# Threshold attention followed by a squared-ReLU MLP: order of the first ten attention steps, and value groups of several blocks

## The chip, the cores and the metric

The kernel runs on one core of a Trainium2 chip. The metric is device time in microseconds (us). Before the change it is 1333.52 us, the median of three runs (1333.27 to 1333.55). All data are float32.

## The reference

Attention over 8 batches and 8 heads, 576 rows each, head width 64, and then a two-layer MLP over the 4608 rows that come out (512 wide, 2048 inside):

```python
scores = q @ k.T / 8
scores = where(scores >= max(scores) - tau, scores, -1e9)
attn = exp(scores - max(scores));  attn /= sum(attn) + 1e-9
x = attn @ v                      # (8, 8, 576, 64) -> rows (8 * 576, 8 * 64)
out = maximum(x @ w_in, 0) ** 2 @ w_out
```

The weights w_in and w_out are handed over as 64-bit words and turned into float32 in the kernel.

## The kernel before

**Visits and steps.** Two heads are handled together, one on partitions 0 to 63 and one on 64 to 127 of the transposed queries (`qT`) and keys (`kT`). A visit is one such pair; a step is one block of 128 query rows of a visit (the fifth block, number 4, has 64 rows of each head and makes one tile of 128). The first sweep goes through the four pairs of batch 0 with blocks 0 and 1 only (visits 0 to 3, steps 0 to 7), the second through the same pairs with blocks 2, 3 and 4 (visits 4 to 7, steps 8 to 19). From visit 8 on a visit has all five blocks (visits 8, 9, 10 are steps 20 to 34). From step 35 on another method, by DMA, turns the weights of attention; the change doesn't touch it.

**One step.** `scores` (L258) multiplies on TensorE (L273) into two PSUM pairs, one for each head, and VectorE takes the row maxima (L310). `exponents` (L319) makes a bias and a threshold on ScalarE from both maxima (L322, L323) and then the exponentials of both heads (L325). `threshold` (L328) drops on VectorE what lies below the threshold and sums the rest, reading scores and exponentials (L337), and makes the reciprocal (L339, L340). `divide` (L342) scales on GpSimd (L345, L347). Two steps later `turn` (L378) transposes the tile on TensorE in three parts of three 128-column pieces (L386), each copied to `wT` by ScalarE (L387; for block 4 L393 to L400). Three steps later `mix` (L499) multiplies with the values (L502), 128 query rows (64 for block 4) in a PSUM bank, and ScalarE copies the result to `xT` (L485). The scores of a step use the same PSUM pairs as those of the step before, so its matmuls wait until L337 has read them; only step 1 has a pair of its own.

**Around a step.** `load_qk` (L171) issues ten loads (four for the queries, six for the keys) on SP's queue, `load_v` (L210) four. `prep` (L232) transposes queries and keys on VectorE (L247), one after the other in the last step of the visit before. `round_weights` turns one of 32 weight pieces into float32: stage 0 is two ScalarE instructions (L149, L150), stages 1 and 2 are VectorE (L152, L154), 3 and 4 GpSimd (L156, L158); in the first sweep there is one piece in the first step of each visit from visit 1 on, later one or two in each step. The next load into the area of a piece is issued when the piece is done (L951).

**The MLP in between.** `chunk_at` says at which step 256 rows of `xT` are complete: chunk 0 at step 10. Before that `early()` is true. From then on `fill` inserts MLP pieces (L548, L730) between the attention's instructions on TensorE. `rate` (L885) spreads the 32 pieces of chunk 0 evenly over the steps until all weights are there (`out_from`, step 34), and what comes later over the rest. The order on each engine is the order in which the program issues; an engine does its instructions in that order.

Of the kernel before, what the change touches and what calls it, by code (L numbers as in the profile page):

```python
# [19 lines left out]
def kernel(  # L20
# [145 lines left out]
    def rows_32(t, n, m):  # L166

        b, h = divmod(visits[n][0], HP)
        return t[b, 2 * h + m // 2, :, (m % 2) * 32:(m % 2) * 32 + 32].rearrange("(c p) d -> p c d", p=32)

    def load_qk(n):  # L171


        for x, t in ((rows_of(n)[1], k), (rows_of(n)[0], q)):
            for m in range(4):
                src, to = rows_32(t, n, m), x[m * 32:(m + 1) * 32, :, :]
                queue = nc.scalar if n == 0 and m % 2 else nc.sync
                last = REST // 32 if t is k and m >= 2 and not by_dma(n) else 0
                queue.dma_start(out=to[:, last:, :], in_=src[:, 0:S // 32 - last, :])
                if last:  # L180
                    queue = nc.gpsimd if n == 0 else nc.sync
                    queue.dma_start(out=to[:, 0:last, :], in_=src[:, S // 32 - last:, :])
# [61 lines left out]
    def prep_part(t, n):  # L244
        to, rows = (qT, rows_of(n)[0]) if t is q else (kT[n % 2], rows_of(n)[1])
        arrived(rows)
        nc.vector.transpose(to, rows.rearrange("p c d -> p (c d)"))  # L247

    def prep_left():
        arrived(q_left)  # L250
# [7 lines left out]
    def scores(s):  # L258


        vis, i = steps[s]
        n = 2 if i < NBLK else 1
        sc = [(second if s == 1 else pairs)[u] for u in range(n)]
        if i == NBLK:
            for half in range(2):
                nc.tensor.matmul(sc[0][:, half, 0:HALF], qmid, kT[vis % 2][:, half * HALF:(half + 1) * HALF], start=True, stop=True)
        else:
            halves = [(half, u) for half in range(2) for u in range(n)]
            if early():
                halves.sort(key=lambda x: x[1])  # L270
            for half, u in halves:
                rows = slice(u * D, (u + 1) * D)
                nc.tensor.matmul(sc[u][:, half, 0:HALF], qT[rows, i * P:(i + 1) * P],  # L273
                                 kT[vis % 2][rows, half * HALF:(half + 1) * HALF], start=True, stop=True)
        maxima(s, [x[:, :, 0:HALF] for x in sc])
# [38 lines left out]
    def keep_busy(times):  # L314

        for x in range(times):
            nc.tensor.transpose(second[1][:, 1, x % 4 * P:x % 4 * P + P], ident, ident)

    def exponents(vis, i):  # L319
        w, sc, st = weights[vis, i]  # L320
# [51 lines left out]
    def keep_bank(what):  # L372
# [2 lines left out]
        kept[what] = used["bank"]  # L375
        return to

    def turn(vis, i, part):  # L378

        w = weights[vis, i][0]  # L380
        ps = take("mm", (6, 7)) if early() and part == 1 else take("tx", (4, 5))
        ps = ps.rearrange("p (c n) -> p c n", n=P)
        if i < NBLK:
            for n in range(3):
                c = 3 * part + n
                nc.tensor.transpose(ps[:, n, :], w.rearrange("p u k -> p (u k)")[:, c * P:(c + 1) * P], ident)  # L386
            nc.scalar.copy(wT[:, 2 * i:2 * i + 2, 3 * part:3 * part + 3, :].rearrange("p g c q -> p c g q"),  # L387
                           ps[:, 0:3, :].rearrange("p c (g q) -> p c g q", g=2))
        elif part < 2:
            rows = slice(part * D, (part + 1) * D)  # L390
            for c in range(NBLK):
                at = part * REST + c * P
                nc.tensor.transpose(ps[:, c, 0:D], w[rows, 0, at:at + P], ident[rows, rows])  # L393
            at = part * (NBLK + 1)
            nc.scalar.copy(wT[:, 2 * NBLK, at:at + NBLK, :], ps[:, :, 0:D])
        else:

            for rows, keys in ((slice(0, D), slice(S - REST, S)), (slice(D, P), slice(0, REST))):
                nc.tensor.matmul(ps[rows, 0, 0:D], w[rows, 0, keys], ident[rows, rows], start=True, stop=True)
            nc.scalar.copy(wT[:, 2 * NBLK, NBLK, :], ps[:, 0, 0:D])  # L400

    blocks = {}
    outside = {}
# [95 lines left out]
    def mix(n, cols):  # L499

        def term(ps, u, c, at, rows=slice(0, P), first=False, last=False):
            nc.tensor.matmul(ps[u * D:(u + 1) * D, :], vs[n % 2][rows, u * (NBLK + 1) + c, :],  # L502
                             wT[rows, at // REST:(at + ps.shape[1]) // REST, NBLK if c == NBLK else u * (NBLK + 1) + c, :],
                             start=first, stop=last)

        above, below = slice(0, D), slice(D, P)
        arrived(vs[n % 2])
        if not by_dma(n):
            ps = take("tx", (4, 5))[:, 0:cols.stop - cols.start]
            for c in range(NBLK + 1):  # L510
                for u in range(2):
                    term(ps, u, c, cols.start, first=(c == 0), last=(c == NBLK))
            put(n, cols.start, ps, False)
            return
        n1, n2 = 2 * P + REST, 2 * P
        at = ODD if paired(n) and n % 2 else ONE
        one, two = bank[0], bank[4]
        groups = (one[:, 0:n1], at, (above, below)), (two[:, 0:n2], TWO, (below, above))
        for ps, x, _ in groups:
            for c in range(NBLK):  # L520
                for u in range(2):
                    term(ps, u, c, x, first=(c == 0))

        for ps, x, places in groups:
            for u, rows in enumerate(places):
                term(ps, u, NBLK, x, rows, last=True)
        put(n, 0, one[:, ONE - at:ONE - at + 2 * P], True)
        left = ODD if at == ODD else LEFT - at
        put(n, NBLK * P, one[:, left:left + REST], False)
        put(n, 2 * P, two[:, 0:n2], True)  # L530
# [305 lines left out]
    for s, (n, i) in enumerate(steps):  # L836

        if by_dma(n):
            mixed = {visits[n][1][-1]: (0, 3 if n % 2 else 4)}
        else:  # L840
            mixed = {x: (x, 3) for x in range(NBLK + 1)}
        if i in mixed:
            first, lag = mixed[i]
            cols = slice(first * P, S if by_dma(n) else min((i + 1) * P, S))
            mixes[s + lag] = (n, cols)
            g_ = visits[n][0]
            if g_ % HP == HP - 1:
                complete[s + lag] = g_ // HP * S + cols.stop
# [6 lines left out]
            j += 1  # L855
    PIECE_US = 1.76
    VALUES_US = 4.8
    SCORES_US = 1.25
    RESERVE = 3 * PIECE_US
    waiting = deque()  # L860
# [24 lines left out]
    def rate(s):  # L885


        if s < out_from:
            return PIECE_US * sum(x[2] == 0 for x in waiting) / (out_from - s)
        have = PIECE_US * len(waiting) - state["left"]  # L890
        best = 1e9
        at = s
        for e in sorted(chunk_at) + [END]:
            if e > s:
                have += sum(other(x) for x in range(at, e))
                at = e
                best = min(best, (have - (RESERVE if e < END else 0)) / (e - s))
                have += PIECE_US * sum(len(pieces_of(x)) for x in chunk_at.get(e, ()))
        return max(best, 0.0) - other(s)

    def other(s):

# [32 lines left out]
    pieces, left = [], n_pieces  # L935
    for s, (n, i) in enumerate(steps):
        if s < HP * FIRST:
            x = int(n > 0 and i == 0)
        else:
            x = 2 if (n, i) in ((2 * HP - 2, FIRST + 1), (2 * HP - 1, FIRST + 1), (2 * HP, FIRST)) else 1  # L940
        pieces.append(min(x, left))
        left -= pieces[-1]
# [59 lines left out]
    for i in range(RAW):  # L1002
        load_weights(i)
    prep(0)
    nc.vector.tensor_scalar(out=ntau8, in0=ntau8, scalar1=-1.0 / SCALE, scalar2=None, op0=ALU.mult)
    keep_busy(20)
    done = 0
    rounded_by = [0]
# [15 lines left out]
    def late_step(s):  # L1024
# [67 lines left out]
        if valued:  # L1092
            at_least(2, made)
            state["left"] = max(state["left"], -PIECE_US / 2)

    for s in range(END + 1):
        state["step"] = s
        if s >= first_late:
            assert 4 not in kept.values()
            late_step(s)  # L1100
# [5 lines left out]
        if on:  # L1106
# [10 lines left out]
                load_qk(n + 1)  # L1117
            if now:
                round_weights(now[0], 0)
            if s != 1:  # L1120
                scores(s)
                after()
                some_later("gpsimd")
        old = steps[s - 2] if 2 <= s < NST + 2 and not by_dma(steps[s - 2][0]) else None
        at_once = now or old or early()
        lay = on and last and more and not by_dma(n) and s != 1
        if old:
            turn(*old, 0)
            turn(*old, 1)
        if on:  # L1130
            exponents(n, i)
            if s and by_dma(steps[s - 1][0]):
# [18 lines left out]
            for j in chunk_at.get(s, ()):  # L1151
                add_chunk(j)
        if old:
            turn(*old, 2)
        state["free"] = s > first_dma
        if s == 0:
            scores(1)
            prep(1)
        smooth = s > first_dma + 2 and s not in mixes
        some_later("vector")  # L1160
        some_later("gpsimd")
# [77 lines left out]
```

## Time and profile before

The profiled execution took 1333.83 us; its span (first to last instruction) is 1332.0 us. A profile shows one execution. "Busy" is the time covered by an engine's instructions; the PE rows are matmuls (PE) and weight loads (PEld).

| | busy us | share of the span | instructions |
|---|---|---|---|
| PE (TensorE matmul) | 1295.4 | 97% | 9112 |
| PEld (TensorE weight load) | 1078.0 | 81% | 9112 |
| DVE (VectorE) | 927.9 | 70% | 2026 |
| ACT (ScalarE) | 583.0 | 44% | 1357 |
| POOL (GpSimd) | 786.0 | 59% | 915 |

The times of a step can be found by its exponentials (L325): step 0 starts them at 11.60 us, step 1 at 13.12, step 2 at 19.90, step 3 at 26.75, step 4 at 31.95, step 9 at 57.93, step 10 at 62.58, step 11 at 68.10. Views that follow name the engine, the line of the program and the tile written; the chain of waits is the list of what ended last, followed back from the end of the program.

### The profile page before, as it was taken

Reading aid. Unit: us, or ns where it says so; the run is one execution under the profiler, and the core shown is the slowest. Engines: PE = TensorE matmul, PEld = TensorE weight load, DVE = VectorE, ACT = ScalarE, POOL = GpSimd, SP = SyncE. Lnnn points to the kernel's source line nnn. Section 1 sums busy time; section 2 is a strip of 40 time slices with the busy share of each in tenths; the row PEclk is TensorE's granted clock in tenths of the full one; section 3 lists DMA queues with packets and bytes.
Section 4 is the critical chain, followed back from the end, with each engine's and each line's share of the span. In section 5 each row is a group of like instructions: output and inputs, shape, how many; then the busy total and the mean of one; then the engine's idle time right before and its main releaser. Section 6 shows DMA issues by size and latency. Waiting matters only on the chain.

```text
span 1332.0 us, 25215 instructions
## 1 busy us (share of the span) xinstructions
PE 1295.4 (97%) x9112; PEld 1078.0 (81%) x9112; DVE 927.9 (70%) x2026; ACT 583.0 (44%) x1357; POOL 786.0 (59%) x915
## 2 busy tenths in 40 slices
PE   7898899999999999999999999999999999999998
PEld 5676556888787979797878878888897988889997
DVE  6877776877777878787777776868687877632131
ACT  4776674235262625343534343434443443421321
POOL 4689875775755565474665665747474747454351
PEclk7999999999999999999999999999999999999999
DMA  8764531648786968776766776676686767520000
GB/s 159 160 153 117 144 91 36 159 111 184 166 196 140 214 152 199 167 172 161 167 155 157 163 179 166 168 149 172 148 186 143 178 150 161 161 70 6 12 17 16
DMA packets 330126, 186.69 MB, mean 140 GB/s; under 512 B 291441, under 2 KB 291473, under 8 KB 323601
## 3 DMA queue, kind: packets, MB, share of 16 engines
q1 hardware_dynamic: 317696, 116.87, 46.5%
q0 software_dynamic: 10000, 67.92, 12.8%
q8 instruction: 72, 1.18, 0.4%
q10 hardware_dynamic: 2304, 0.29, 0.2%
q14 instruction: 54, 0.43, 0.1%
HBM read 109.22 MB, written 68.42 MB: 133 GB/s over the span
## 4 chain that ended last, share of the span: by engine, by line
PE 86%; DVE 4%; ACT 3%; POOL 2%; DMA 2%; issue 1%; SPq 0%; ACTq 0%; DVEq 0%; POOLq 0%
PE big L659 29%; PE big L765 28%; PE big L502 10%; PE big L289 8%; PE big L548 3%; PE big L273 3%; PE big L730 2%; PE big L386 2%; DVE st L310 1%; ACT wT L387 1%; DMA wT<-aside 1%; DVE w L337 1%; ACT w L325 1%; DMA aside<-turned 1%; POOL w L347 1%
## 5 line engine op out<-in xcount | busy, mean ns | idle before, releaser
L337 DVE SCALAR_TENSOR_TENSOR w<-big,st,w 128x576 f32<-128x576 f32 x269 | 207.1, 805 | 96.8 <-ACT w L325 96.5
L310 DVE TENSOR_REDUCE st<-big 128x1 f32<-128x576 f32 x288 | 204.2, 748 | 93.8 <-PE big L289 61.7
L347 POOL TENSOR_SCALAR w<-w,st 128x576 f32<-128x576 f32 x269 | 246.6, 926 | 26.4 <-DVE st L340 21.4
L765 PE MATMUL big<-wo,gsum 128*128 128x256 f32 x1088 | 243.8, 382 | 0.0
L765 PEld LDWEIGHTS big<-wo,gsum 128*128 128x128 f32 x1088 | 204.4, 190 | 37.0 <-issue 8.1
L659 PE MATMUL big<-xT,w_in_sb 128*128 128x128 f32 x1536 | 187.4, 277 | 1.3 <-DVE g L671 1.2
L659 PEld LDWEIGHTS big<-xT,w_in_sb 128*128 128x128 f32 x1536 | 178.5, 192 | 10.6 <-issue 8.1
L765 PE MATMUL big<-wo,g 128*128 128x256 f32 x816 | 185.3, 382 | 0.1
L325 ACT ACTIVATE w<-big,st 128x576 f32<-128x576 f32 x269 | 183.8, 734 | 0.0
L765 PEld LDWEIGHTS big<-wo,g 128*128 128x128 f32 x816 | 151.6, 190 | 26.1 <-issue 6.5
L502 PE MATMUL big<-wT,vs 128*64 128x128 f32 (+5 forms) x1700 | 164.2, 355 | 8.3 <-ACT wT L387 4.2
L502 PEld LDWEIGHTS big<-wT,vs 128*64 128x64 f32 (+1 forms) x1700 | 97.1, 137 | 72.0 <-issue 20.7
L322 ACT ACTIVATE st<-st 128x2 f32<-128x2 f32 (+1 forms) x148 | 30.3, 205 | 258.2 <-DVE st L310 257.1
L345 POOL TENSOR_SCALAR st<-st 128x2 f32<-128x2 f32 (+1 forms) x148 | 35.2, 238 | 169.3 <-DVE w L337 163.5
L408 POOL DMA_DIRECT2D aside<-turned x50 | 29.9, 597 | 177.9 <-DVE turned L437 173.7
L671 DVE TENSOR_TENSOR g<-big,g 128x512 f32<-128x512 f32 x96 | 64.7, 676 | 82.4 <-PE big L659 76.8
L289 PE MATMUL big<-kT,qT 64*128 64x256 f32 (+3 forms) x768 | 106.9, 416 | 0.0
L289 PEld LDWEIGHTS big<-kT,qT 64*128 64x128 f32 x768 | 84.5, 186 | 14.5 <-issue 5.0
L667 ACT ACTIVATE g<-g 128x512 f32<-128x512 f32 x96 | 60.2, 628 | 62.9 <-DVE g L671 62.7
L538 POOL TENSOR_TENSOR gsum<-g 128x512 f32<-128x512 f32 x34 | 46.2, 1358 | 69.8 <-ACT g L668 69.6
L668 ACT ACTIVATE g<-g 128x512 f32<-128x512 f32 x128 | 80.7, 630 | 4.1
L431 DVE STREAM_TRANSPOSE turned<-w 128x512 f32<-128x512 f32 x100 | 70.2, 702 | 0.0
(114 smaller groups left out, 2039.0 us busy)
## 6 DMA issues: line engine op xcount, KB each, us to landing
aside<-turned POOLq DMA_DIRECT2D x50, 1152.0 KB, 4.8
wT<-aside SPq DMA_DIRECT2D x200, 288.0 KB, 5.4
vs<-in_v_dram SPq DMA_DIRECT2D x72, 128.0 KB, 6.1
ql<-in_q_dram SPq DMA_DIRECT2D x126, 72.0 KB, 5.0
wo<-in_moe_w_in_dram SPq DMA_DIRECT2D x16, 512.0 KB, 4.6
wo<-in_moe_w_out_dram SPq DMA_DIRECT2D x16, 512.0 KB, 3.8
out_dram<-osb POOLq DMA_DIRECT2D x32, 256.0 KB, 3.6
kl<-in_k_dram SPq DMA_DIRECT2D x113, 72.0 KB, 2.9
```

Source lines behind the costliest of these rows:

```text
L289: nc.tensor.matmul(big[to, at + x0:at + x1], lhsT, keys[u * D:(u + 1) * D, x0:x1], start=True, stop=True)
L310: nc.vector.tensor_reduce(out=mx[:, u:u + 1], in_=sc[u], axis=AX.XY, op=ALU.max)
L325: nc.scalar.activation(out=w[:, u, :].rearrange("p (h k) -> p h k", h=2), in_=sc[u], func=AF.Exp, bias=bias[:, u:u + 1], scale=SCALE)
L337: nc.vector.scalar_tensor_tensor(out=wu, in0=sc[u], scalar=thr[:, u:u + 1], in1=wu, op0=ALU.is_ge, op1=ALU.mult, accum_out=sm[:, u:u + 1])
L347: nc.gpsimd.tensor_scalar(out=w[:, u, :], in0=w[:, u, :], scalar1=z[:, u:u + 1], scalar2=rcp[:, u:u + 1], op0=ALU.add, op1=ALU.mult)
L431: move(wb[:, 0:h, :, :], whole_[:, 0, :, :, :])
L502: nc.tensor.matmul(ps[u * D:(u + 1) * D, :], vs[n % 2][rows, u * (NBLK + 1) + c, :], wT[rows, at // REST:(at + ps.shape[1]) // REST, NBLK ...
L659: nc.tensor.matmul(to[:, f, :], factor(j, p, q, c)[:, f * P:(f + 1) * P], part[:, c, :], start=(p in "125" and f == 0 and c == 0), stop=(p ...
L667: nc.scalar.activation(out=to, in_=to if src is None else src, func=AF.Relu)
L668: nc.scalar.activation(out=to, in_=to, func=AF.Square)
L671: nc.vector.tensor_tensor(out=x, in0=to, in1=x, op=ALU.add)
L765: nc.tensor.matmul(to, left[:, f, :], wo[:, slot, f, :], start=(f == 0), stop=(f == HF - 1))
```

## The change

It has these parts.

1. The steps with `early()` (0 to 9) are issued by a new function, `early_step`. The exponentials of the first head are issued before the bias of the second (`early_exponents`); the threshold is made by VectorE for both heads. The copies of the turned parts are held back by `turn` as functions and issued after the exponentials, and all three parts of `turn` go before `mix`. `turn` and `mix` take their banks from 4, 5, 6 and 7 in turn while `early()` holds. The heads' matmuls are sorted by head in steps 0 and 1 only; in the other steps they alternate.
2. Keys of the next visit are transposed in the first step of a visit and queries in the second, ahead of L337 (before: both in the last step, ahead of L337). Queries are loaded and transposed only for the columns that the sweep needs: 256 of 576 in the first sweep, 320 in the second. The keys of visit 0 are transposed in two halves. The negated tau is made by GpSimd.
3. A weight piece of the first sweep starts (stage 0) in the second step of a visit, after the copies, and its later stages follow at the end of the next step; in step 9 those of two pieces.
4. From visit 4 on `mix` handles several blocks at once: 2, 3 and 4 of a visit of the second sweep (320 columns), 0 and 1, 2 and 3, and 4 of visits 8, 9 and 10. `wT` gets places by visit for that (`place_of`). Chunk 1 is therefore complete at step 22 instead of 21.
5. `rate` counts 1.1 us for 128 columns of values until `out_from`, so that fewer MLP pieces go into steps with values and more into the others.

```diff
+    def columns(t, n):
+        first = FIRST * P // 32
+        return slice(0, S // 32) if t is k or n >= 2 * HP else slice(0, first) if n < HP else slice(first, S // 32)
...
-                queue.dma_start(out=to[:, last:, :], in_=src[:, 0:S // 32 - last, :])
+                queue.dma_start(out=to[:, cols.start + last:cols.stop, :], in_=src[:, cols.start:cols.stop - last, :])
...
-        nc.vector.transpose(to, rows.rearrange("p c d -> p (c d)"))
+        for x in (slice(0, HALF // 32), slice(HALF // 32, S // 32)) if t is k and n == 0 else (columns(t, n),):
+            nc.vector.transpose(to[:, x.start * 32:x.stop * 32], rows[:, x, :].rearrange("p c d -> p (c d)"))
...
-            if early():
+            if s < 2:
                 halves.sort(key=lambda x: x[1])
...
+    def early_exponents(vis, i):
+        w, sc, st = weights[vis, i]
+        nc.vector.tensor_scalar(out=st[:, 1, :], in0=st[:, 0, :], scalar1=ntau8, scalar2=None, op0=ALU.add)
+        for u in range(len(sc)):
+            bias = st[:, 2, u:u + 1]
+            nc.scalar.activation(out=bias, in_=st[:, 0, u:u + 1], func=AF.Copy, scale=-SCALE)
+            nc.scalar.activation(out=w[:, u, :].rearrange("p (h k) -> p h k", h=2), in_=sc[u],
+                                 func=AF.Exp, bias=bias, scale=SCALE)
...
+    def place_of(n, i):
+        return n % 2 * 4 + 2 * i if n < HP else n % 2 * 5 + 2 * (i - FIRST) if n < 2 * HP else 2 * i
...
-        ps = take("mm", (6, 7)) if early() and part == 1 else take("tx", (4, 5))
+        to = place_of(vis, i)
+        ps = take("tx", (4, 5, 6, 7) if early() else (4, 5))
...
-            nc.scalar.copy(wT[:, 2 * i:2 * i + 2, 3 * part:3 * part + 3, :].rearrange("p g c q -> p c g q"),
+            return lambda: nc.scalar.copy(wT[:, to:to + 2, 3 * part:3 * part + 3, :].rearrange("p g c q -> p c g q"),
...
-            mixed = {x: (x, 3) for x in range(NBLK + 1)}
+            mixed = {x: (x, 3) for x in range(FIRST)} if n < HP else {NBLK: (FIRST, 3)} if n < 2 * HP else {1: (0, 3), 3: (2, 3), NBLK: (NBLK, 3)}
...
-            return PIECE_US * sum(x[2] == 0 for x in waiting) / (out_from - s)
+            return (PIECE_US * sum(x[2] == 0 for x in waiting) + sum(early_values(x) for x in range(s, out_from))) / (out_from - s) - early_values(s)
...
-            x = int(n > 0 and i == 0)
+            x = int(n > 0 and i == 1)
...
+    def early_step(s):
+        n, i = steps[s]
+        first = i == visits[n][1][0]
+        now = list(range(sum(pieces[:s]), sum(pieces[:s + 1])))
+        if first and n + 2 < 2 * HP:
+            load_qk(n + 2)
+        if s != 1:
+            scores(s)
+            early_exponents(n, i)
+        copies = [turn(*steps[s - 2], part) for part in range(3)] if s > 1 else []
+        if s == 0:
+            scores(1)
+            early_exponents(*steps[1])
+        elif n < HP and s > 1:
+            prep_part(k if first else q, n + 1)
+        if not first:
+            split_left(n)
+        for fn in copies:
+            fn()
+        if s in mixes:
+            mix(*mixes[s])
+        for p in now:
+            round_weights(p, 0)
+        threshold(n, i)
+        if s == 0:
+            prep(1)
+        divide(n, i)
+        rounding.extend(now)
+        while rounding and (rounding[0] not in now or s == min(chunk_at) - 1):
+            p = rounding.popleft()
+            for stage in (1, 2, 3):
+                round_weights(p, stage)
+            end_rounding(p)
+        if first and n:
+            load_v(n)
```

In the diff `turn`'s other two copies are returned as functions in the same way, and the steps from 10 on call them at once, where they stood.

## The prediction

> **What bounds the kernel now.** I read the page first (TensorE 97% busy), then the busy times of stretches that I cut at the steps' exponentials (cells: busy us and instructions of PE, PEld, DVE, ACT, POOL; granted clock, DMA share, GB/s):
>
> ```profile
> 0.00:62.28 62.28, 47.93 (x326) 36.12 (x328) 44.84 (x103) 36.57 (x89) 31.28 (x54) 0.89 0.80 158
> 62.28:95.00 32.72, 31.15 (x266) 24.09 (x262) 23.69 (x52) 24.71 (x62) 27.21 (x31) 1.00 0.64 152
> 95.00:150.00 55.00, 48.83 (x384) 35.55 (x384) 44.26 (x92) 38.45 (x96) 47.21 (x49) 1.00 0.45 128
> 150.00:206.00 56.00, 54.03 (x405) 33.07 (x406) 40.20 (x95) 40.01 (x100) 44.24 (x49) 1.00 0.44 105
> ```
>
> TensorE idles 14.4 us up to step 10, when the MLP begins, and 6.2 us in 95 to 150 us, where GpSimd is nearly full. Elsewhere it has work without pause, and after 206 us its work is not changed. So the change is worth what it takes from the ten first steps, plus what TensorE work it takes from later stretches that TensorE bounds. Next the chain of waits, one step of the first ten:
>
> ```profile
> 31.95 0.75 ACT wo L325
> 32.72 0.84 DVE wo L337 x2
> 33.60 1.97 PE big L273 x7
> 35.57 0.49 PE big L386 x3
> 36.09 0.86 ACT wT L387 x2
> 36.95 0.10 ACT st L322
> 37.05 0.05 ACT st L323
> 37.14 0.75 ACT w L325
> ```
>
> The step takes 37.14 - 31.95 = 5.19 us, and the two copies of turned parts stand between the maxima and the exponentials. The same 5.19 to 5.20 us recur up to step 9. VectorE's own content sets the floor under it.
>
> **Steps 4 to 9 when warm.** Let 0 be the start of the first L337 of a step. By the timeline the second starts at 0.74, sum and reciprocal end at 1.9; TensorE is let into the first head's bank at 0.88 (33.60 - 32.72) and into the second's at 1.62. With heads alternating, pairs of matmuls run side by side at 0.245 us a pair (read in the timeline from 108.56 us on), the first head is done about 0.8 after 1.62, and its maximum starts at 2.42. Two maxima of 0.70, the threshold 0.15 (a 128x1 operation took 0.11, a 128x2 reciprocal 0.17), and the transpose: keys 0.68, or 256 columns of queries 0.35 (0.77 by 256/576). Then L337 can start: 4.65 with keys. With queries the two L152 and L154 of a piece come before the maxima (start 2.60): 4.50. ScalarE's way is shorter: maximum 0.73, bias 0.27, exponential to L337 0.78, so 4.2 to 4.4. TensorE has scores 1.24, nine transposes 1.2 and values 1.31, ending at 5.2 where the next bank comes free at 5.46. Copies (1.3 us) and, in second steps, a piece's 1.37 us on ScalarE end at 7.7, just before the next bias at 7.8. Mean step 4.58: steps 5 to 9 gain 5 x (5.19 - 4.58) = 3.0 us. If the alternating heads don't overlap, the first head is done 0.5 later and a step takes 4.9 (gain 1.4); the floor by VectorE's content is 4.47 (3.6).
>
> **The start.** Queries of visit 0 shrink by 164 KB, some 1.0 us at 160 GB/s (0.3 to 1.4), and the first scores wait for 0.36 + 0.37 us of transposes instead of 1.49: 1.6 us earlier. But step 2 now transposes the keys of visit 2, ahead of its L337; before, that came a step later:
>
> ```profile
> 12.88 2.77 SPq L179 DMA_DIRECT2D kl<-in_k_dram  x3
> 17.52 1.14 SPq L182 DMA_DIRECT2D kl<-in_k_dram  x1
> 25.97 0.73 DVE L247 STREAM_TRANSPOSE kT<-kl 128x576 f32<-128x576 f32 x1
> ```
>
> The last key load of visit 2 is issued at 17.52; loads of this form took 3.8 us to land, so about 21 us. VectorE would get there at about 18.0. Moved past SP: the issue order of ten query and key loads, four of values and three of weights stays, and so does their number, so smaller queries don't move 12.88. Here the Trainium skill speaks against the change: "DMA: Bandwidth & Descriptors" (Issuing engines are not separate DMA queues; Queues, rings and completion order) has all loads share 16 engines and each engine take descriptors in ring order, so these keys stand behind the three weight loads of 1.5 MB issued just before. This trace agrees: 365 GB/s are moved from 14.6 to 18.0 us, and the first key loads took 6.5 us. By the rule the keys land at 20.5 to 21 as before and step 2's L337 starts at 21.3 instead of 20.66 (0.6 lost); by VectorE's row alone it would start at 18.7 (1.9 won). I take the rule.
>
> Then the clock:
>
> ```profile
> 11.00:14.60 3.60, 0.00 (x0) 0.00 (x0) 3.60 (x8) 3.19 (x8) 0.00 (x0) 1.00 0.73 167
> 14.60:18.00 3.40, 3.30 (x10) 2.25 (x11) 3.12 (x13) 1.25 (x2) 2.07 (x4) 0.52 1.04 365
> 25.00:28.40 3.40, 3.40 (x26) 2.74 (x25) 2.58 (x6) 2.53 (x6) 2.68 (x3) 0.50 0.78 132
> 28.40:31.80 3.40, 3.40 (x29) 2.59 (x31) 2.73 (x7) 2.81 (x8) 1.85 (x3) 1.00 0.82 216
> ```
>
> TensorE stood still for 3.6 us and then ran at half clock from 14.6 to 28.4. The new order has such a pause too (about 9.5 to 14.5, and 19.5 to 22). "TensorE: Matmul & The Clock Gate" (Part 1) gives full clock back after one busy window of some 3.4 us. By the trace (cold to 28.4) step 3's transposes and values of step 0 end at 28.5, scores of step 4 follow, and its L337 starts at 31.8; by the rule, warm from about 26, at 30.8. Before: 32.72. I take 31.3: 1.4 us gained at step 4, all losses above included.
>
> **The hand-over at step 10.** What was moved behind comes due here. After step 9's exponentials ScalarE had one turned copy, a piece and two copies before step 10's; now it has three copies and two pieces: 2 x 0.43 + 1.37 = 2.2 us more. VectorE's L152 of step 9's own piece waits for them too, with the maxima of step 10 behind it, and GpSimd has 2.5 us more. Cost 2.4 us. Sum at step 10: 1.4 + 3.0 - 2.4 = 2.0 us earlier (bounds -1.5 and 5). From here TensorE is full in both kernels, so this shift stays.
>
> **Merged values.** The nearest rows are the later visits (320 and 256 columns in one piece of the chain) against single groups of 128 and 64:
>
> ```profile
> 325.14 4.72 PE big L502 x38
> 105.18 1.24 PE big L502 x20
> 170.88 0.73 PE big L502 x20
> ```
>
> 576 columns in two groups cost 4.72, so 320 cost 2.65 with 0.03 of overhead and 256 cost 2.12. A visit of the second sweep falls from 1.24 + 1.24 + 0.73 = 3.21 to 2.65 (0.56), one of visits 8 to 10 from 5.69 to 4.97 (0.72). Where TensorE bounds (visits 4 and half of 5, half of 7, and 8 to 10) that is 2 x 0.56 + 3 x 0.72 = 3.3; in 95 to 150 a third of the remaining 1.1, 0.4. TensorE's waits for a copy before L502 (3.8 us in the two full stretches) fall by about 0.6. A lump of 2.65 us in one step delays the scores behind it by up to 1.9 us; `rate` takes one piece out of that step, and I charge 0.5 in all. Sum 3.8 (0 to 6).
>
> The rest costs nothing: the second sweep's shorter query transposes lie on VectorE (44 of 55 us busy); if that cover went they would gain 0.3 each. Chunk 1 one step later is hidden, since it is not touched before `out_from`. Next load of a weight piece: ordered by ScalarE's stage 0, two steps ahead of its use.
>
> **Sum.** 1333.83 - 2.0 - 3.8 = 1328.0 in a profiled execution; that stood 0.3 above the median, so 1327.7.
>
> **Rivals.** *The start goes well* (keys land by 19, clock warm by 26, hand-over under 1 us): 2 + 1 + 1.5 more, and if TensorE's waits in 95 to 150 fall with the values gone from two steps of three, another 2: 1321. For it: VectorE has nothing else to wait for; against it: 17.52 and the 3.8 us. *Nothing is left*: the hand-over and late keys eat steps 5 to 9, and merging is hidden in a stretch paced by GpSimd's rounding: 1333. For it: 47 of 55 us of GpSimd. *Slower*: the lump. In 95 to 150 us a step's scores, maxima and exponentials start a chain through GpSimd that the next scores wait for. If each of the four visits of the second sweep pays the full 2.65 - 0.73 = 1.9 us in its last step, and the 1.24 us groups taken away were covered, that is +7.6, against 2.0 and the 2.2 of visits 8 to 10: 1337. It decides from 1.05 us a visit. Against it: before that step's scores `fill` leaves out one piece of 1.76 us.
>
> **Chances and range.** Differences under 0.2% (2.7 us) are what a measurement of this kernel can hardly tell. Forecast (1324 to 1330.8) 0.55, good start (1318 to 1324) 0.22, nothing left 0.14, slower 0.09. Faster 0.77, same 0.15, slower 0.08: a tenth of the slower case's chance lies inside the bound. The range takes in most of the good start and of nothing left: 1320 to 1333; the forecast's own is 1324 to 1330.8.
>
> **What would show it.** In the chain of steps 4 to 9: L387 gone, VectorE (L310, L247, L337) in its place, 4.5 to 4.7 us from one step's first L325 to the next's; step 2's transpose L247 waiting for a load of `kl`; half clock to 26 to 28 us; step 10's exponentials some 7 us behind step 9's (62.58 - 57.93 = 4.65 before) with L149 and L387 ahead of them; L502 groups of 320 columns at 2.65. I am wrong if keys land by 18 us, if L273 takes over 1.9 us in steps 4 to 9, or if TensorE's idle time in 95 to 150 us changes by more than 2 us.

## The result: 0.4% faster, by other terms than forecast

The changed kernel took 1328.62 us (median of five runs, 1327.58 to 1329.52), the kernel before 1333.55 us in the same session (1333.27 to 1335.45). The ratio is 0.9963, with a 95% interval of 0.9952 to 0.9975. The forecast was 1327.7, so the total was right to 0.9 us. Its terms were not, and most of this text is about that.

The profiled execution took 1328.56 us. The head of its page and its engine row (busy us, share of the span, instructions):

```profile
span 1326.8 us, 24669 instructions
PE 1289.0 (97%) x8832; PEld 1066.5 (80%) x8832; DVE 936.7 (71%) x2036; ACT 582.3 (44%) x1343; POOL 787.9 (59%) x916
```

There are 280 matmul instructions fewer (9112 before), which is the merging, and TensorE is busy 6.4 us less. The span is 5.2 us shorter (1332.0 before). To see where, both kernels are cut at the same four events: the first exponentials of steps 10, 16, 24 and 34. Cells as in the prediction: busy us and instructions of PE, PEld, DVE, ACT, POOL, then granted clock, DMA share, GB/s; the number after the limits is the length. The kernel before:

```profile
0.00:62.58 62.58, 48.23 (x332) 36.42 (x334) 45.14 (x104) 36.87 (x91) 31.49 (x55) 0.89 0.80 158
62.58:98.24 35.66, 33.25 (x290) 25.72 (x287) 26.57 (x60) 27.23 (x69) 28.25 (x31) 1.00 0.64 155
98.24:151.35 53.11, 46.94 (x374) 34.13 (x372) 41.85 (x84) 36.98 (x92) 47.31 (x50) 1.00 0.43 121
151.35:208.70 57.35, 55.98 (x422) 34.52 (x420) 41.46 (x98) 40.36 (x101) 44.90 (x51) 1.00 0.43 103
```

The changed kernel:

```profile
0.00:63.34 63.34, 45.16 (x332) 33.36 (x334) 48.61 (x114) 37.62 (x90) 32.13 (x57) 0.89 0.63 135
63.34:97.64 34.30, 31.61 (x204) 23.82 (x202) 26.58 (x60) 26.91 (x65) 29.33 (x30) 1.00 0.69 167
97.64:147.09 49.45, 46.78 (x274) 30.75 (x272) 43.36 (x83) 36.79 (x86) 47.26 (x50) 1.00 0.44 130
147.09:202.90 55.81, 53.98 (x336) 31.00 (x334) 43.01 (x99) 39.73 (x98) 44.44 (x49) 1.00 0.43 106
```

| stretch | before us | after us | difference | forecast |
|---|---|---|---|---|
| start to step 10 | 62.58 | 63.34 | +0.8 | -2.0 |
| step 10 to 16 | 35.66 | 34.30 | -1.4 | |
| step 16 to 24 | 53.11 | 49.45 | -3.7 | |
| step 24 to 34 | 57.35 | 55.81 | -1.5 | -3.8 for the three |
| step 34 to the end of the span | 1123.3 | 1123.9 | +0.6 | 0 |

The first ten steps, for which most of the code was written, lose 0.8 us. The stretches behind them, with the merged values and the new spread of MLP pieces, win 6.6. The largest gain lies in steps 16 to 24, the stretch in which GpSimd sets the pace, where the forecast gave almost nothing: TensorE's idle time there falls from 53.11 - 46.94 = 6.2 us to 49.45 - 46.78 = 2.7 us. GpSimd is busy for the same time in both, 47.31 and 47.26 us, so all of the 3.7 us is time in which it stood idle (5.8 us before, 2.2 after). In the two other stretches TensorE's busy time falls by 1.6 and 2.0 us, which is as much as they gain.

**The first ten steps in lines.** Here is step 5 of the changed kernel, a second step of a visit, on VectorE (timeline: start us, us, engine, line, operation, tiles):

```profile
33.96 0.41 DVE L152 TENSOR_SCALAR turned<-turned 128x512 uint32<-128x512 uint32 x1
34.40 0.94 DVE L154 TENSOR_SCALAR turned<-turned 128x512 uint32<-128x512 uint32 x1
35.27 1.40 DVE L317 TENSOR_REDUCE st<-big 128x1 f32<-128x576 f32 x2
36.71 0.60 DVE L329 TENSOR_SCALAR st<-st,ntau 128x2 f32<-128x2 f32 x1
37.22 0.43 DVE L254 STREAM_TRANSPOSE qT<-wo 128x256 f32<-128x256 f32 x1
37.58 0.77 DVE L354 SCALAR_TENSOR_TENSOR w<-big,st,w 128x576 f32<-128x576 f32 x1
```

and GpSimd at the same time:

```profile
34.24 1.80 POOL L364 TENSOR_SCALAR wo<-wo,st 128x576 f32<-128x576 f32 x2 [0.28 <-DVE st L357]
36.01 1.27 POOL L156 TENSOR_TENSOR turned<-turned 128x512 f32<-128x512 f32 x1
```

L154 does the same on the same shape as L152 and takes 0.94 us instead of 0.41. It starts inside the first of the two L364 (0.83 us, to about 35.1) and ends at 35.34, 0.3 us behind it; the second L364, which starts meanwhile, takes 0.99 us. L329 is an operation on two numbers in each partition; it starts at 36.71, inside L156 (36.01 to 37.28), and is over at 37.31, when L156 is. VectorE is held by GpSimd twice, for 0.5 and 0.4 us, and both operations stand ahead of the step's first L354. From one first L354 to the next, second steps (5, 7 and 9) take 5.46, 5.52 and 5.49 us and first steps (6 and 8) 4.81 and 4.23 (steps 8 and 9 have no transpose). By the exponentials steps 4 to 9 take 25.78 us; before, 25.98.

The hand-over at step 10, on ScalarE:

```profile
60.05 0.68 ACT turned L149
60.74 0.57 ACT turned L150
61.30 0.56 ACT turned L149
61.86 0.56 ACT turned L150
62.42 0.75 ACT wT L409 x2
...
63.45 0.64 ACT wo L342
```

Two pieces and the turned copies stand ahead of step 10's exponentials (chain of waits; in the timeline the exponentials start at 63.34), which start 6.79 us behind step 9's instead of 4.65.

**The paced stretch in lines.** The chain of waits in the kernel before, up to the scores of step 18 (visit 7). The line left out is "105.18 1.24 PE big L502 x20", which the prediction shows:

```profile
103.15 1.28 POOL w_in_sb L158
104.48 0.70 PE big L548 x2
...
106.42 0.48 PE big L386 x3
106.90 1.73 PE big L548 x8
108.63 1.17 PE big L273 x8
```

and the same place in the changed kernel:

```profile
101.41 2.51 POOL w_in_sb L158 x2
103.97 0.70 PE big L571 x2
104.67 0.33 PE big L408 x3
105.00 1.73 PE big L571 x8
106.72 1.22 PE big L280 x8
```

A weight piece is finished by GpSimd (L158), an MLP piece has waited for it (L548, now L571), and the scores (L273, now L280) that start GpSimd's next round stand behind it on TensorE. A round is three steps here. In the kernel before a group of values stands between, on the chain; after the change that step has none. The round from 98.24 to 118.05 us (19.81 us) becomes 97.64 to 116.32 us (18.68 us), 1.1 us less.

That is not yet the 3.7 us. In steps 19 to 22 the same pattern returns in the kernel before: a group of values (124.92 us in the timeline) stands between a piece that waited for L158 and the scores. It is gone after the change, and the three steps take 17.78 us instead of 18.95. But the chain of waits runs over GpSimd itself there, so the group is the likely cause and not a shown one. Steps 22 to 24 get 1.4 us shorter. GpSimd's long waits between 98 and 152 us are these two before (a third takes 0.36 us):

```profile
116.80 2.63 POOL L156 TENSOR_TENSOR turned<-turned 128x512 f32<-128x512 f32 x2 [1.37 <-DVE turned L154]
142.66 2.56 POOL L156 TENSOR_TENSOR turned<-turned 128x512 f32<-128x512 f32 x2 [2.61 <-DVE turned L154]
```

and after the change:

```profile
115.07 2.63 POOL L156 TENSOR_TENSOR turned<-turned 128x512 f32<-128x512 f32 x2 [0.36 <-DVE turned L154]
139.43 2.61 POOL L156 TENSOR_TENSOR turned<-turned 128x512 f32<-128x512 f32 x2 [0.36 <-DVE turned L154]
```

The first wait, 1.0 us shorter, ends the round above. The second, 2.3 us shorter, lies in step 22. On what it depends was not isolated: the MLP's operations on GpSimd have moved as well (one on the tile `g`, 1.04 us, stands at 138.03 just ahead of this wait after the change; before, the next one came behind it, at 147.27).

### The profile page after: what moved, and what is told of

It is laid out like the page before. It is cut to its first block, busy times and chain, and to the rows that moved or that the text cites. A ratio compares the mean times of both kernels' runs of the same rounds, so it can differ in the third digit from the quotient of the medians.

```text
span 1326.8 us, 24669 instructions
## 1 busy us (share of the span) xinstructions
PE 1289.0 (97%) x8832; PEld 1066.5 (80%) x8832; DVE 936.7 (71%) x2036; ACT 582.3 (44%) x1343; POOL 787.9 (59%) x916
## 4 chain that ended last, share of the span: by engine, by line
PE 83%; DVE 4%; DMA 3%; ACT 2%; POOL 1%; issue 1%; SPq 0%; DVEq 0%; POOLq 0%
PE big L682 29%; PE big L788 28%; PE big L524 10%; PE big L296 8%; PE big L571 3%; PE big L280 2%; DMA wT<-aside 2%; PE big L753 1%; DVE st L317 1%; DMA aside<-turned 1%; PE big L408 1%; DVE w L354 1%; ACT w L342 1%; ACT wT L409 1%; PE big L273 0%
## 5 line engine op out<-in xcount | busy, mean ns | idle before, releaser
L354 DVE SCALAR_TENSOR_TENSOR w<-big,st,w 128x576 f32<-128x576 f32 x269 | 207.2, 806 | 88.6 <-ACT w L342 88.1
L364 POOL TENSOR_SCALAR w<-w,st 128x576 f32<-128x576 f32 x269 | 246.5, 925 | 27.3 <-DVE st L357 22.6
L342 ACT ACTIVATE w<-big,st 128x576 f32<-128x576 f32 x255 | 174.1, 733 | 0.2 <-issue 0.2
L524 PE MATMUL big<-wT,vs 128*64 128x256 f32 (+5 forms) x1420 | 159.5, 389 | 7.6 <-ACT wT L409 4.2
L524 PEld LDWEIGHTS big<-wT,vs 128*64 128x64 f32 (+1 forms) x1420 | 86.3, 136 | 72.4 <-issue 19.3
```

What stands on the lines that cost most here:

```text
L342: nc.scalar.activation(out=w[:, u, :].rearrange("p (h k) -> p h k", h=2), in_=sc[u], func=AF.Exp, bias=bias[:, u:u + 1], scale=SCALE)
L354: nc.vector.scalar_tensor_tensor(out=wu, in0=sc[u], scalar=thr[:, u:u + 1], in1=wu, op0=ALU.is_ge, op1=ALU.mult, accum_out=sm[:, u:u + 1])
L364: nc.gpsimd.tensor_scalar(out=w[:, u, :], in0=w[:, u, :], scalar1=z[:, u:u + 1], scalar2=rcp[:, u:u + 1], op0=ALU.add, op1=ALU.mult)
```

## Experiments

Two theories stood after the result. **A**: the gain comes from the later stretches, that is from the merged values and `rate`, and the new first steps bring nothing to the end. **B**: the first steps carry a good part of it. All ratios are to the kernel before in the same session; its median there was 1333.91, 1334.18 or 1335.53 us. Every run computes the whole output.

**The new first steps alone.**

```diff
-            mixed = {x: (x, 3) for x in range(FIRST)} if n < HP else {NBLK: (FIRST, 3)} if n < 2 * HP else {1: (0, 3), 3: (2, 3), NBLK: (NBLK, 3)}
+            mixed = {x: (x, 3) for x in range(NBLK + 1)}
...
-    EARLY_VALUES_US = 1.1
+    EARLY_VALUES_US = 0.0
```

> The changed kernel with values of one block each again and without the 1.1 us in rate: the first ten steps and the shorter queries alone. Theory A (read from the two traces: step 10's exponentials come 0.8 us later than before, all of the gain comes from the values): 1333 to 1335 us, step 10's exponentials at 63.3 us. Rival B (the first ten steps are worth the 2.0 us of the prediction, only seen later): 1331 to 1332 us.

Measured: 1335.13 us, ratio 1.0009 (1.0003 to 1.0016). The first ten steps alone are no gain; they end 0.6 us later at step 10 (63.22) and it stays (0.9 us at step 34). A holds and B falls.

**The merged values alone**, in the loop of the kernel before: `mixed`, `place_of` and `rate` of the change, `early_step` left out.

```diff
-            mixed = {x: (x, 3) for x in range(NBLK + 1)}
+            mixed = {x: (x, 3) for x in range(FIRST)} if n < HP else {NBLK: (FIRST, 3)} if n < 2 * HP else {1: (0, 3), 3: (2, 3), NBLK: (NBLK, 3)}
...
+    EARLY_VALUES_US = 1.1
...
-            return PIECE_US * sum(x[2] == 0 for x in waiting) / (out_from - s)
+            return (PIECE_US * sum(x[2] == 0 for x in waiting) + sum(early_values(x) for x in range(s, out_from))) / (out_from - s) - early_values(s)
```

> The kernel before with merged values, their places and the new rate, and the old first ten steps. Theory A: all of the gain and a little more, 1326.5 to 1328.5 us, step 10's exponentials at 62.6 us as before. Rival B: the 3.8 us of the prediction for the values, 1329.5 to 1330 us.

Measured: 1333.03 us, ratio 0.9994 (0.9986 to 1.0002). Neither theory: here the gain is missing too. The sum of the two parts is nothing, and together they give 0.4%. The reason is in how MLP pieces fall into the steps. These are TensorE's pieces in steps 16 to 19 of each kernel, in order (a dot is a part of `turn`, i a piece of L571, V1, V2 and V5 values of 64, 128 and 320 columns):

```
step                    17        18        19
before               .iV2.i     .V2.i     .V1.i

step           16        17        18        19
changed       .V5.     .i.i      .i.i      .V5.
merged alone  .V5.     .i.ii     ..i       .V5.
rate 0        .V5.i    .i.i      ..i       .V5.i
```

In the loop of before, `fill` is called in the steps before 10 as well, and with the new `rate` it adds to its account there, before any piece exists. So the account is fuller when chunk 0 comes, and step 17 gets three pieces. The chain of waits of this run, at the place shown above:

```profile
100.84 1.28 POOL w_in_sb L158
102.16 0.70 PE big L554 x2
102.86 0.33 PE big L391 x3
103.19 3.46 PE big L554 x16
106.64 1.17 PE big L273 x8
```

3.46 us of pieces stand ahead of the scores, where the changed kernel has 1.73. The values are gone from the chain, and a second piece has taken their place. GpSimd's two waits for L154 are 2.61 and 2.62 us here. The clock adds up to 1.7 us in this profile: it was at half at about 143 to 147 us.

**The merged values alone, with the pieces where the changed kernel has them.** The previous run, and one line more:

```diff
+        if s < min(chunk_at):
+            return 0.0
         if s < out_from:
```

> The kernel before with merged values, their places and the new rate, and with rate 0 until step 10, so that every MLP piece stands in the same step and place as in the changed kernel. Theory P (where the pieces stand decides; the first ten steps only shift): step 10's exponentials at 62.6 us and the whole 0.5 to 1.2 us faster than the changed kernel, 1327.4 to 1328.1. Theory Q (the new first ten steps are needed for the gain): 1332 to 1333 us, as with the pieces at other places.

Measured: 1329.99 us, ratio 0.9966 (0.9953 to 0.9978), as good as the whole change at 0.9963; that it is 0.5 to 1.2 us better, as theory P had it, does not show. Step 10 starts at 62.41 here, and the stretch from step 16 to 24 takes 49.30 us, as in the changed kernel (49.45), with GpSimd's two waits at 0.36 us each. So the places of the pieces were what the run before lacked, and the new first steps contribute nothing that can be measured.

**The changed kernel without the 1.1 us in `rate`.**

```diff
-    EARLY_VALUES_US = 1.1
+    EARLY_VALUES_US = 0.0
```

> The changed kernel with 0 instead of 1.1 us for 128 columns of values in rate (merged values stay). Theory A1 (steps without values are what shortens the stretch paced by GpSimd): up to 1 us slower than the changed kernel, 1328.5 to 1329.5 us. Theory A2 (fewer MLP pieces in steps with values shorten it): 3 us slower, 1331 to 1332 us.

Measured: 1339.45 us, ratio 1.0040 (1.0027 to 1.0052), some 10 us above the changed kernel by the two ratios; both expectations were far too small. Now a piece stands in the step of the 320-column group (`.V5.i` above), in front of the next scores. The chain of waits from 97 us on:

```profile
100.08 3.27 PE L524 MATMUL big<-wT,vs 128*64 128x320 f32 x20
103.67 1.89 PE L571 MATMUL big<-xT,w_in_sb 128*128 128x256 f32 x8
105.49 1.24 PE L280 MATMUL big<-kT,qT 64*128 64x288 f32 x8
```

This is the forecast's slower rival, the lump: values, a piece and only then the scores. Part of the loss is the clock. In this run it fell to half twice between 96 and 122 us; part of one of the two stretches (cells as above):

```profile
98.00:100.00 2.00, 2.00 (x8) 1.35 (x7) 1.75 (x5) 0.45 (x1) 1.60 (x2) 0.50 0.74 219
```

Both together cost at most 3.4 us (their length times the clock missing). The rest, some 7 us, I put down to the places of the pieces, by the chain; it was not separated further.

**The 1.1 us in `rate` with values one block at a time**, to complete the square: the changed kernel with the first edit of the first experiment alone.

> The changed kernel with values of one block each again; rate keeps its 1.1 us. Theory A1: 4 to 5 us slower than the changed kernel, 1333 us. Theory A2: only the TensorE time of the groups is lost, some 2.5 us (seven visits at 0.35), 1331 us.

Measured: 1333.21 us, ratio 0.9995 (0.9987 to 1.0004). With the new first steps in all four:

| | `rate` 0 | `rate` 1.1 us |
|---|---|---|
| values one block at a time | 1.0009 | 0.9995 |
| values merged | 1.0040 | 0.9963 |

Merging without `rate` costs 0.3%, `rate` without merging is worth 0.1%, and both together 0.5%. The gain is theirs together.

**Why did the first steps not get faster?** Theory: VectorE is held by GpSimd in the second steps (L154 and L329 above). The next run moves both away from GpSimd's operations: ScalarE makes the threshold, and L152 and L154 are issued ahead of L354.

```diff
-        nc.vector.tensor_scalar(out=st[:, 1, :], in0=st[:, 0, :], scalar1=ntau8, scalar2=None, op0=ALU.add)
...
+            nc.scalar.activation(out=st[:, 1, u:u + 1], in_=st[:, 0, u:u + 1], func=AF.Identity, bias=ntau8)
...
+        ready = list(rounding)
+        for p in ready:
+            round_weights(p, 1)
+            round_weights(p, 2)
         threshold(n, i)
...
-            for stage in (1, 2, 3):
+            for stage in (3,) if p in ready else (1, 2, 3):
```

> The changed kernel with the threshold made by ScalarE again (one instruction for each head) and with L152 and L154 of a piece ahead of the step's threshold, where GpSimd is idle. Theory S (VectorE's L154 takes 0.94 instead of 0.41 us and its threshold 0.60 instead of 0.23 us because GpSimd works at the same time, and VectorE sets the step): two steps take 9.3 to 9.5 us instead of 10.3, step 9's exponentials come 2 to 2.7 us earlier, and so does the end: 1326 to 1326.7 us. Rival (another engine paces these steps): step 9's exponentials within 0.7 us of 56.55.

Measured: 1328.60 us, ratio 0.9955 (0.9943 to 0.9968). VectorE in steps 4 and 5 of this run:

```profile
32.40 0.39 DVE L152 TENSOR_SCALAR turned<-turned 128x512 uint32<-128x512 uint32 x1
32.82 0.43 DVE L154 TENSOR_SCALAR turned<-turned 128x512 uint32<-128x512 uint32 x1
35.58 1.42 DVE L317 TENSOR_REDUCE st<-big 128x1 f32<-128x576 f32 x2 [0.47 <-PE big L280]
37.73 0.82 DVE L354 SCALAR_TENSOR_TENSOR w<-big,st,w 128x576 f32<-128x576 f32 x1 [0.38 <-ACT w L333]
```

L154 is back at 0.43 where GpSimd is idle, and two steps take 9.7 to 10.0 us instead of 10.3. Expected were 9.3 to 9.5, and step 9's exponentials come 0.86 us earlier, not 2 to 2.7 and just past the rival's 0.7. So the hold is a real term, but about half of what was missing to the forecast's 4.65 + 4.50 is still there. The last two lines show why: the run pays for what it takes away. L152 and L154 had stood where VectorE would wait for the scores, and now it waits there, for 0.47 us, in second steps too; and ScalarE has one instruction more ahead of each head's exponentials, for which VectorE waits in step 5. So this run doesn't measure the hold alone, and as both edits were made at once, their shares are not separated. The 0.86 us are given back at step 10 (63.80): TensorE waits 2.36 us there, and the clock falls to half for the step's work.

```profile
59.77 2.26 PE L273 MATMUL big<-kT,qmid 128*128 128x288 f32 x4 [2.36 <-DVE w L354]
```

This L273 takes 1.24 us in the changed kernel.

**Keys of visit 2 ahead of the weights.** The late keys are taken away by their place on SP's queue.

```diff
     load_qk(1)
+    prep(0)
+    load_qk(2)
     load_v(0)
...
-    prep(0)
...
-        if first and n + 2 < 2 * HP:
+        if first and 0 < n and n + 2 < 2 * HP:
```

> The changed kernel with the loads of visit 2's queries and keys ahead of the first values and the three weight loads on SP's queue. If step 2 waits for its keys behind the weights, its first L354 starts at 19.6 to 20.0 us instead of 20.99 and the wait of 1.2 us is gone; the end 0 to 1.2 us earlier. If something else held it, it stays at 20.99.

Measured: 1328.38 us, ratio 0.9953 (0.9939 to 0.9967). In the changed kernel VectorE waits 1.23 us in step 2 (timeline; the releaser named is the last load of that queue):

```profile
20.29 0.78 DVE L254 STREAM_TRANSPOSE kT<-kl 128x576 f32<-128x576 f32 x1 [1.23 <-DMA ql<-in_q_dram]
20.99 0.78 DVE L354 SCALAR_TENSOR_TENSOR w<-big,st,w 128x576 f32<-128x576 f32 x1
```

Here the transpose starts at 19.67 without the wait, L354 at 20.38 (19.6 to 20.0 was expected), and steps 4 to 10 are 1.3 us earlier. It is given back between steps 11 and 12: the clock falls to half between 62 and 68 us, and the scores there take 2.29 us.

**Both together.** Each of the two was worth about 1 us at step 9 and nothing at step 12.

> Both of the two before it together. If what is won in the first ten steps reaches the end: sum of the two, step 9's exponentials at 53 us, 1325 to 1326.5 us. If the later stretches give it back: 1328 us.

Measured: 1324.74 us, ratio 0.9929 (0.9917 to 0.9942), faster than the changed kernel (their intervals don't meet). Step 9 starts at 51.67 instead of 56.55 and step 10 at 59.04 instead of 63.34. At step 9 the two gains together (4.9 us) are more than their sum (2.2), and the clock, which comes back earlier, goes with it. Granted clock in the third column from the right, 20 to 25 us, the changed kernel:

```profile
20.00:25.00 5.00, 3.17 (x9) 2.02 (x10) 3.40 (x9) 1.19 (x4) 1.85 (x3) 0.50 0.52 83
```

and with both edits:

```profile
20.00:25.00 5.00, 4.68 (x39) 3.30 (x39) 4.30 (x12) 3.62 (x12) 1.85 (x3) 1.00 1.00 249
```

What is won before step 10 does reach the end: 4.3 us at step 10, 4.7 at step 34, 5.0 in the span (1321.8). But the early return of the clock is not sure: the last run below has the same order up to step 7, had 0.66 from 20 to 25 us in its profile, and began step 4 0.9 us later. The forecast's assumption that a shift at step 10 stays was right here.

**The clock alone.** In the changed kernel TensorE pauses 5.3 us after the scores of step 1. Eighteen transposes of the identity, whose results nobody reads, fill part of it (a pause of 3 us remains).

```diff
         if s == 0:
+            for x in range(18):
+                nc.tensor.transpose(pairs[0][:, 0, x % 2 * P:x % 2 * P + P], ident, ident)
             prep(1)
```

> The changed kernel with 18 transposes of the identity on TensorE between the scores of step 1 and of step 2 (into the bank that step 0's first threshold has read), so that TensorE stands still for 3 instead of 5.3 us there. If that pause is what halves the clock until 28 us: granted clock 1.00 from 15 us on, step 4's exponentials at 28.5 to 29.5 us instead of 30.77, the end 1 to 2 us earlier. If the clock falls anyway: step 4 at 30.8 us, the end unchanged.

Measured: 1328.05 us, ratio 0.9948 (0.9936 to 0.9961). The clock is 0.91 from 20 to 25 us instead of 0.50, but step 4 starts only 0.6 us earlier (30.17). Expected were 28.5 to 29.5 with a full clock, or 30.8 if the clock fell anyway; it is neither. That the end is earlier than the changed kernel's is not shown, since the intervals overlap. Step 2's transpose waits for its keys here too (0.86 us), and its L354 comes at 21.09, as in the changed kernel: the keys hold step 2, not the clock.

**All three.**

> Early keys, the threshold on ScalarE, L152 and L154 ahead, and those 18 transposes. If the clock of the version without them (full from 20 us on) came from its shorter pauses: 0.3 to 1 us better than that version (ratio 0.992 to 0.9927); if it is full there by chance, no difference.

Measured: 1324.00 us, ratio 0.9917 (0.9903 to 0.9930), the best version run. The clock stays full through the start:

```profile
15.00:20.00 5.00, 2.69 (x20) 1.73 (x18) 4.86 (x13) 2.01 (x7) 2.94 (x5) 1.00 0.73 187
```

Step 4 starts at 27.16 (30.77 in the changed kernel). That it beats the two edits without the transposes is not shown: the intervals overlap.

**The hand-over two steps earlier.** The two edits of "both together", with the new steps only to step 7 and the old order for steps 8 and 9.

```diff
-        while rounding and (rounding[0] not in now or s == min(chunk_at) - 1):
+        while rounding and (rounding[0] not in now or s == 7):
...
-        if early():
+        if s < 8:
```

> Early keys, the threshold on ScalarE, L152 and L154 ahead, and the old order already from step 8 on, so that the work moved behind comes due at step 8. If the hand-over costs its 2.2 us wherever it stands: step 10's exponentials within 0.7 us of the 59.04 us of the version with ten new steps. If it is the second piece of step 9 that costs: 1.5 to 2.5 us earlier.

Measured: 1328.46 us, ratio 0.9952 (0.9938 to 0.9965). Steps 7 to 8 and 8 to 9 take 7.0 and 6.9 us instead of 4.5 and 4.6, step 9 to 10 takes 4.9 instead of 7.4, and step 10 starts at 62.24 instead of 59.04. Neither expectation came true. Of these 3.2 us 0.9 were there at step 4, by the clock. Up to 1.7 more may be the clock's too: behind a pause of 2.35 us it was at half twice as long as in the version with ten new steps (from 52 to 60 us it was 0.56, 0.50, 0.50 and 0.73, in pieces of 2 us). What is left, 0.6 us, would fit a toll that costs the same wherever it stands; that it can be avoided by paying earlier is not shown, nor that it can't. The MLP pieces stand elsewhere in this run, so its end says nothing on the toll alone.

## Why the prediction was right, and where it was not

**Start: right.** It gave 1.4 us at step 4; 31.95 became 30.77, 1.2 us. Step 2's L354 was forecast at 21.3 behind late keys and came at 20.99. The rule from "DMA: Bandwidth & Descriptors" that was taken against VectorE's own row (18.7) held, and the run with the keys ahead of the weights shows the cause. The clock was forecast at half to 26 to 28 us; it was 0.50 from 15 to 25 and 0.75 from 25 to 30.

**Warm step 4.58 us: wrong, it is 5.16.** This is the first step that failed. "Then L337 can start: 4.65 with keys. With queries ... 4.50." Keys took 4.81, queries 5.5. The sum added VectorE's durations as if nothing but its own order bound them. Two terms were mis-sized: L154 at its short size of 0.41 (0.94 measured) and the threshold, 0.15 from the nearest row of that size (0.60). The trace of before could have warned: L154 there ranges from 0.41 to 1.32 us and L152 from 0.41 to 1.50, the long ones beside GpSimd instructions (the longest beside L158, at 64.48 us); in its first ten steps most were short. The Trainium skill states the rule: "SBUF — State Buffer" (Who interferes with whom) has VectorE and GpSimd share a port pair that one instruction holds to its end while the other waits, when VectorE runs in a two-port mode, and "VectorE: DVE Perf Modes" (Mode 2×_2P) has a single-source 4-byte operation in SBUF run in such a mode. L154 and L329 are of that kind, and they end 0.3 us or less behind GpSimd's instruction; the maxima and L354, which read PSUM, keep 0.70 and 0.77 us beside GpSimd. With the two sizes as measured the query step comes out at 4.50 + 0.53 + 0.45 = 5.48, and steps 5 and 7 took 5.46 and 5.52. The run without the two conflicts won back only 0.3 to 0.7 us of two steps, because of the waits that it brought. Gain of steps 5 to 9: 0.2 us instead of 3.0.

**Hand-over 2.4 us: right.** 6.79 - 4.65 = 2.14. Ahead of step 10's exponentials ScalarE has three copies, two pieces and two more copies; the forecast's list of them leaves out the last two, but its 2 x 0.43 + 1.37 counts them. With the terms above, -1.18 - 0.20 + 2.14 = +0.76 at step 10, as measured. That this shift stays was right to step 34 (62.41 against 63.34 at step 10, 201.78 against 202.90 at step 34, in the run with the merged values alone and the pieces in their places). At the end of the span the two are equal (1326.9 and 1326.8): the stretch from step 34 to the end takes 1123.1 to 1125.1 us in the profiles of all kernels, and a single microsecond cannot be followed that far.

**Merged values, TensorE's work: a size off.** 320 columns were put at 2.65 and 256 at 2.12, from 4.72 for 576. One of the groups of the changed kernel (timeline):

```profile
174.61 2.38 PE L524 MATMUL big<-wT,vs 128*64 128x256 f32 x20 [0.24 <-ACT wT L409]
```

From a group's start to the start of the next work 320 columns take 2.84 and 256 take 2.31 (128 and 64 took 1.24 and 0.73). On a line through these four a group costs 0.2 us by itself, whatever its width; that is worked out from these runs. The two groups of 576 columns take only 4.72 by the same measure, so dividing them left the 0.2 out. A visit saves 3.21 - 2.84 = 0.37 or 5.69 - 5.35 = 0.34, not 0.56 and 0.72: 2.5 us for the seven visits.

**"In 95 to 150 a third of the remaining 1.1, 0.4": wrong, 3.7.** This is the second step that failed. It took the stretch as GpSimd's, with TensorE's work hidden. But the very line from which values were priced, "105.18 1.24 PE big L502 x20", was a line of the chain in this stretch: GpSimd's round starts from scores that stand behind a piece and values in TensorE's order. Taking this one group from the path shortened the round by 1.1 us (GpSimd's wait from 1.37 to 0.36). The next three steps, where such a group is gone too, got 1.2 us shorter and steps 22 to 24 another 1.4. Places of MLP pieces change there as well, the runs don't separate the two, and so the cause of these 2.5 us stays open. The rival "values gone from two steps of three, another 2" had the mechanism of the first part and was given to a lesser chance. The counter-run is the merged values with two pieces in that place: 3.46 us on the chain and no gain.

**The lump, 0.5 us: right only with `rate`.** With the 1.1 us in `rate` no loss shows; without, some 10 us, more than the slower rival's 7.6. Its mechanism was real, and "before that step's scores `fill` leaves out one piece" was the right reason against it.

So the total came out because an error of +2.8 us in the first ten steps (0.8 instead of -2.0) met one of -2.2 us behind them (-6.0 instead of -3.8). That is luck, and the mark given in advance for being wrong, TensorE's idle time in 95 to 150 us changing by more than 2 us, was passed (3.5 us).

## What to carry to other kernels

That an engine has idle time does not mean that its work is hidden: where the pacing engine's next round starts from an instruction that stands behind other work in a fuller engine's order, that work is on the path, and the chain of waits says so line by line. When a change moves work between steps, count what the planner puts in its place, since the same edit was worth 0.4%, nothing or a loss by the places of two MLP pieces. And before adding up an engine's durations, look at the spread of each row: a row whose longest is three times its shortest (0.41 and 1.50 us here) may be held by another engine, and the new order decides whether that happens.

## What the runs showed of the hardware that I had not expected

- An operation on two numbers in each partition (L329, shortest 0.23 us) took 0.60 us beside a GpSimd operation, and one of 128x512 (0.41 us) took 0.94 and up to 1.50 (L152 of the kernel before). The wait is inside the instruction's own duration; it is not shown as idle time with a releaser.
- The clock fell to half behind pauses of TensorE of 2.30 to 2.36 us in five runs (the threshold moved, the keys first, both, all three, and the earlier hand-over), and behind 2.19 and 3.05 us without the 1.1 us in `rate`. Behind the same 2.30 us (and the same 1.10 us before it) it stayed full in the changed kernel, in both runs with the new first steps and single values, and with the transposes alone. In the merged values alone it stayed full behind 3.23 us (until 113.99) and fell at about 143 us behind 1.28 us. So the length of the pause alone doesn't decide. Each fall was worth 1.7 us (lengths of the stretches times the clock missing), which is 3.4 us at half clock; the one of the earlier hand-over was twice that. "TensorE: Matmul & The Clock Gate" (Part 1) speaks of a free-running window of some 3.4 us, which would fit. No run moved the pause against a window, so this is not shown.
- Transposes of the identity kept the granted clock up: 1.00 from 10 to 25 us in the best version, though TensorE was busy for only 5.2 of the 10 us from 10 to 20, the transposes among them. Without them the version with both edits had 0.66 from 15 to 20 us. These are single profiles.
